# The fifth channel tile of an Infini-attention kernel: summed in one bank per 64-row half instead of in two halves of its columns, with a rewritten order

## The chip, the cores and the metric

The kernel runs on one core of a Trainium2 chip, as one launch. The metric is the device time of one execution in microseconds (us); before the change the median of three runs is 519.08 us (518.57 to 522.13).

## What is computed

A token gate mixes two branches of the same input x (2048 tokens of 640 channels). Branch a is Infini-attention with 32 heads of 20 channels over 4 segments of 512 tokens: within a segment softmax attention with a mask, plus a read of a memory that the earlier segments left. Branch b sends one token through a gated feed-forward network and adds the result to it.

```
q, k, v = (x @ wq, x @ wk, x @ wv), each cut into 32 heads of 20 channels
for s in range(4):                                   # segments of 512 tokens
    p = softmax(qs @ ks.T * scale + mask);  a_dot = p @ vs
    a_mem = (phi(qs) @ M) / (phi(qs) @ z + 1e-6)
    o = g * a_mem + (1 - g) * a_dot
    M += phi(ks).T @ vs;  z += phi(ks).sum()
a = o @ wo;   b = x + (one token through the network)
out = gate * a + (1 - gate) * b
```

## The kernel before, in words

The heads are taken in two halves of 16, and each half runs over the four segments, so the work falls into 8 units, u = 0 to 7. A unit projects x on its queries and keys (channels on the partitions, 512 tokens on the columns), on its values (tokens on the partitions), and runs four groups of four heads through the attention. All projections and the products of queries and keys work with numbers split into a high and a low part: hi*hi, lo*hi and hi*lo are summed, so each product is three matmuls.

TensorE is used as two halves of 64 rows (r = 0 and 1) that run at the same time, with two matmuls that start together (a pair, below). Both may not write one PSUM bank at the same time. PSUM is four pairs of banks (`banks`, 128 x 2 x 512 float32 each); an accumulation takes a whole pair or one bank of it.

The queries and keys of a unit are 640 channels, five tiles of 128. `t_job` (L700) sums them over KT = 5 blocks of input channels: tiles 0 and 1 together ("P1"), 2 and 3 together ("P2"), and tile 4 alone ("T4"). `paired` (L646) issues the matmuls, all of them at L665. It goes over the five blocks twice (`by_phase`): in phase 0 half r writes bank r, in phase 1 it writes bank 1 - r, so that after both phases each bank has the sum over all rows. For P1 and P2 bank b holds tile j0 or j1, with 512 columns. For T4 there is one tile only, so its 512 columns are cut, and bank b holds 256 of them:

```
b = r ^ ph
xh, xl = (t.t[:, 256 * b:256 * b + 256] for t in (xh, xl))        # if j0 == j1
```

Between the phases, the two halves change banks, and no half may write into a bank in which the other is still at work. Where the order gives no other proof of that, a poke is planned (L653): VectorE copies two numbers out of the pair into `nil`, after phase 0, and the first matmul of phase 1 waits for it.

`evac_t` (L767) takes a tile out: ScalarE copies it from PSUM to `xs` (L779; for T4 from both banks, 256 columns each, L777), and the pair is free. For P1 of unit 0 alone, which `first_job` (L675) sums into two pairs, VectorE adds the second pair to `xs` (L782). GpSimdE then rounds `xs` to its high part `hi` (L430) and subtracts to get the low part `lo` (L434), and SyncE's queue sends both to DRAM (`stk`), from where `fetch` (L861) brings them back laid out by head. Behind the first segments `phi` is made from `xs` too (L787 to L789).

The attention's matmuls are L903 (products for the row maxima, which VectorE reduces at L909 and L914), L953 (products for the exponentials, which ScalarE takes at L959), L986 (p @ v), L824 and L845 (the memory's read and write). The feed-forward network runs beside them, and 16 output jobs (`o_job`, 320 columns a matmul) close the program.

Nothing of the order is left to a scheduler. Every operation is a task with a number, the string ORDER lists all tasks in the order in which they are issued (L99 to L199), and BANKS gives the bank of each accumulation as it is opened; `Plan.order` (L307) reads both. Each engine runs its tasks in that order.

Of the kernel before, what the change touches and what calls it, by code (L numbers as in the profile page):

```python
# [103 lines left out]
62 7a 5m 5k 61 6d 7x 6m 6e 5y 6f 3g 55 9s 39 75 7b 56 5o 5z 7c 5n 5r 7d 70 76 6h 7e 53 60 6i 5u 5p 7f 5s 6z 7g 8h 6j 6y b 71
7h 3h 8i 6r 7i 5w 77 8v 7j 78 hh 6k 8w ad 6l 9d 72 ae 7m 9v 6x 7k 73 9e 9w 7n 6w 7l 74 9t 9x 9u 7o 65 7y 7p 9y 67 66 6n is 7z
9z c 7q 5v 68 7r 80 a0 7s a1 69 81 6o 6s 5x 7t 6p a2 7u 3d a3 6q a4 3e 3j 8b 82 3b a5 8c 6a 8d 83 54 bv 8f j ce 6t 8e bw 3c c6
3i 9b 84 57 87 3k bx 9a 88 3l 3m 86 cb 3a 89 85 by 58 59 cj h 99 c7 8a bz cc f cf 8x 98 6u 3n be 8y 3o 3p b3 c0 16e 3q g 8o cg
3r c1 90 b5 6v c2 8p c9 c8 bf 91 b6 c3 8r 92 hi 8j 16c 8s c4 8k 8t ck 9f 8l c5 9g 8m e0 9i e1 9h 8n e2 eb k 93 8z e3 94 ej e4
96 95 8q 9j 9m e5 97 a6 9l e6 9n cl b4 e7 9k e8 9p 9o ca e9 a7 ea ch cd fz ci ga 9q a8 g0 a9 9r g1 ec b7 g2 b8 g3 aa as g4 ba
b9 de g5 ab at g6 ed df ac bb g7 av bd af d bc ek g8 dc eg g9 ag el ii aw al ef ax hd ee ah ai e eo i au he bo am aj bp ak bg  # L110
bm bh ay dg az bi bj b1 b0 eh bn bq di bk dh b2 an dj dk ao cu dd ap dm br bl gb ep hq hj dl fp d1 fn cv cm d2 bs fm h2 bu h3
bt d4 d3 en h4 cn em d5 dn h5 d6 cp co h6 do gc cq h7 du cr h8 dq h9 dv dr eq d7 ha d8 dt dx hb da d9 hr ds hc db ij dy hs er
jn jm aq fw j1 dz es r6 ks ge cs fx eu et ar ft fo ik kt ev ct fu fb fv ey ew id fc j4 dp ex ie j5 dw fe fy j6 ic it ez ff iu
ib f4 fg f1 1b7 j2 gf j3 gg gi f5 f2 j7 gj fd f3 j8 3f gl gv fh j9 gm cw fi f6 ja gw fj go fl cx gp ei jb gy gx fk gn gq jc gd
s9 cy gz fq gs f7 gr jd f8 fr gk fs h1 je h0 f0 gt i0 lm ht gu lu ln i1 lo cz i3 d0 il sj hu lb kg im i4 hk lp lc r7 i5 io ld
r8 hl ip le iq lv hn lf 16f lx lw ir ke ho iv lg jf hp lh iw i2 lq in li f9 iy ix jg i6 lj gh ku fa kh iz ji hm lk j0 jh lz ll
i7 m0 i9 jj i8 hf o6 mz ia jl jk o7 mx if hv ly hw ju hx kf lr hy ls n0 ny lt hg nz k3 ig nn k4 no o1 o0 jv np o9 nq k6 nr o2
jo kl ns ss k7 jp nt hz k8 nu nv jr nw km js nx jt po ko pp pz pq jw q0 kp k9 pr ka kr kn ps kc kb jx ih kq l4 jq rf l1 l5 my
jy ki m1 kd l7 l6 m8 l2 pt mv jz kv l8 pu kw l3 q2 la mw pv m9 l9 o3 pw kx pc px ky k5 py o8 pe kz m2 r2 mb l0 ob oa oc k0 m3
# [78 lines left out]
2l2  # L198
"""  # L199
BANKS = ("624062406064202660264610406400264025046272624620466012402460622006246026061246204226016214602405435620462442604407420654"  # L200
         "224027460462461024260762067602406206205402476046034242064270436742603420440622454623404260542406262462040476256240746054"
         "262043042046432603423760204606246704266023642066235604264406470263460302402654224670362024662612406202432074260205064042"
         "6651562044042000642")

# [1123 lines left out]
```

## Time and profile before

| | |
|---|---|
| median of three runs | 519.08 us (518.57 to 522.13) |
| the profiled execution | 519.61 us |
| its span, first to last instruction | 517.9 us |
| granted TensorE clock over the span | 0.998 |
| PE busy | 508.5 us, 98% |
| weight loads (PEld) busy | 409.7 us, 79% |
| VectorE (DVE), ScalarE (ACT), GpSimdE (POOL) busy | 416.6, 407.4, 335.2 us |

Times in the profile count from the span's start. L12 is line 12 of the kernel. "out<-in" are the program's names for what an instruction writes and reads, without buffer numbers. An idle time is followed by what ended it. PE's matmuls are pipelined and their ends modelled, so a busy PE may still have lost time between two starts; the distance from one start to the next is the better measure of its pace. DVE is VectorE, ACT ScalarE, POOL GpSimdE, SP the queue that issues DMAs.

### The profile page before, as it was taken

How to read it: one execution, taken by the hardware profiler on the slowest of the kernel's cores; microseconds unless marked ns; L12 is line 12 of the kernel's file. 1: busy time of each engine (PE TensorE's matmuls, PEld its weight loads, DVE VectorE, ACT ScalarE, POOL GpSimd, SP SyncE). 2: the span in 40 equal slices, each digit the busy share in tenths (PEclk: the TensorE clock that was granted, in tenths of full speed). 3: DMA queues.
4: the chain of work that ended last, by engine and by line, in shares of the span. 5: the costliest groups of instructions: out<-in, count | busy, mean ns of one | idle time of the engine just before them, and what ended most of it. 6: DMA issues, size and time to landing. Idle time of an engine off the chain costs nothing.

```text
span 517.9 us, 17296 instructions
## 1 busy us (share of the span) xinstructions
PE 508.5 (98%) x6916; PEld 409.7 (79%) x6916; DVE 416.6 (80%) x727; ACT 407.4 (79%) x701; POOL 335.2 (65%) x439
## 2 busy tenths in 40 slices
PE   8999999999999999999999999999999999999996
PEld 5998967877777877687778777777778688787896
...
GB/s 253 266 258 212 205 218 223 195 261 212 146 187 255 243 213 244 235 261 242 248 256 230 290 257 216 297 244 235 252 295 213 263 251 251 241 162 183 188 161 130
DMA packets 57712, 119.02 MB, mean 230 GB/s; under 512 B 6240, under 2 KB 13920, under 8 KB 57632
## 3 DMA queue, kind: packets, MB, share of 16 engines
...
## 4 chain that ended last, share of the span: by engine, by line
PE 89%; DVE 3%; DMA 2%; ACT 2%; POOL 1%; issue 1%; SPq 0%; DVEq 0%; ACTq 0%; POOLq 0%
PE bank L665 49%; PE bank L986 13%; PE bank L953 8%; PE bank L903 7%; PE bank L824 4%; PE bank L845 3%; DMA ffn<-in_wg_dram 1%; PE bank L806 1%; ACT pt L959 1%; PE bank L691 1%; DVE mx L914 1%; DMA pt<-in_xT_dram 1%; POOL pt L961 1%; DVE pt L1212 1%; PE bank L926 1%
## 5 line engine op out<-in xcount | busy, mean ns | idle before, releaser
L959 ACT ACTIVATE pt<-bank 128x1024 f32<-128x1024 f32 x160 | 163.1, 1023 | 43.9 <-PE bank L953 39.5
L914 DVE TENSOR_REDUCE mx<-bank 128x2 f32<-128x256 f32 (+2 forms) x192 | 160.8, 859 | 24.1 <-PE bank L903 17.0
L961 POOL TENSOR_SCALAR_AFFINE_SELECT pt<-pt 128x512 f32<-128x512 f32 (+1 forms) x160 | 96.4, 618 | 66.5 <-ACT pt L959 65.1
L665 PE MATMUL bank<-xhi,whi 64*128 64x512 f32 (+1 forms) x460 | 87.8, 364 | 0.0
L665 PE MATMUL bank<-xhi,wlo 64*128 64x512 f32 (+1 forms) x460 | 84.6, 350 | 0.6 <-DVE wlo L434 0.6
L896 ACT CAST bank<-cau 128x512 f32<-128x512 bf16 (+1 forms) x160 | 81.0, 508 | 5.0 <-PE bank L894 1.5
L665 PE MATMUL bank<-xlo,whi 64*128 64x512 f32 (+1 forms) x460 | 84.7, 351 | 0.0
L434 POOL TENSOR_TENSOR xlo<-raw,xhi 128x512 fp32r<-128x512 f32 x53 | 69.5, 1323 | 22.4 <-ACT xhi L428 16.0
L986 PE MATMUL bank<-pt,va 128*32 128x512 f32 (+3 forms) x1024 | 75.5, 435 | 0.6 <-POOL pt L961 0.6
L953 PE MATMUL bank<-qs,ks 62*128 62x256 f32 (+3 forms) x512 | 68.7, 327 | 1.9 <-ACT kk L811 0.8
L903 PE MATMUL bank<-ks,qs 60*128 60x512 f32 (+3 forms) x512 | 69.5, 321 | 0.0
L986 PEld LDWEIGHTS bank<-pt,va 128*32 128x32 f32 x1024 | 30.4, 110 | 43.4 <-issue 34.0
L665 PE MATMUL bank<-vhi,xhi 64*128 64x322 f32 (+1 forms) x320 | 56.6, 323 | 0.1
L953 PEld LDWEIGHTS bank<-qs,ks 62*128 62x128 f32 x512 | 45.6, 185 | 12.9 <-issue 2.6
L665 PE MATMUL bank<-vlo,xhi 64*128 64x322 f32 (+1 forms) x320 | 53.9, 307 | 0.0
L665 PE MATMUL bank<-vhi,xlo 64*128 64x322 f32 (+1 forms) x320 | 53.9, 307 | 0.0
L434 POOL TENSOR_TENSOR lo<-xs,hi 128x512 fp32r<-128x512 f32 x40 | 53.0, 1327 | 1.3
L903 PEld LDWEIGHTS bank<-ks,qs 60*128 60x128 f32 x512 | 47.4, 186 | 6.6 <-ACT bank L896 1.4
L665 PE MATMUL bank<-whi,xhi 64*128 64x320 f32 x320 | 51.0, 312 | 0.0
L665 PEld LDWEIGHTS bank<-xlo,whi 64*128 64x128 f32 x460 | 46.5, 184 | 5.2
L665 PEld LDWEIGHTS bank<-xhi,wlo 64*128 64x128 f32 x460 | 46.8, 186 | 4.5 <-POOL wlo L434 0.8
L665 PE MATMUL bank<-whi,xlo 64*128 64x320 f32 x320 | 50.0, 305 | 0.0
...
## 6 DMA issues: line engine op xcount, KB each, us to landing
stk<-hi SPq DMA_DIRECT2D x40, 512.0 KB
...
```

The source lines that it names most:

```text
L434: plan.add(engine, dur, lambda: e.tensor_tensor(out=lo, in0=src, in1=f32(hi), op=OP.subtract), key, [*reads, hpart], [lpart], lazy=engine ...
L665: nc.tensor.matmul(t[:, b, :n], w[64 * r:64 * r + 64], m[64 * r:64 * r + 64], start=i == 0 and p == 0, stop=ends and p == 2, skip_group_ch ...
L691: nc.tensor.matmul(t[:, b, c], w[k].t[64 * r:64 * r + 64, 128 * b:128 * b + 128], m.t[64 * r:64 * r + 64, c], start=k == 0 and p == 0, sto ...
L824: nc.tensor.matmul(t[32 * j:32 * j + 32, ps.bank, :], mbd.t[:, g, 32 * j:32 * j + 32], e.t, start=True, stop=True)
L845: nc.tensor.matmul(t[32 * m:32 * m + 32, ps.bank, :GW], kk.t[:, g, c, 32 * m:32 * m + 32], v.t[:, c, GW * pos:GW * pos + GW], start=c == 0 ...
L896: act(key, acts(256 * d), lambda: nc.scalar.copy(sub(banks[ps.pair], at_, [[512, 2], [pitch, d], [1, 128]]), sub(cau.t, 0, [[0, 2], [0, d] ...
L903: nc.tensor.matmul(a[:, b, to:to + w], q.t[64 * b:64 * b + ST, p, 128 * i:128 * i + 128], sub(k.t[64 * b:64 * b + ST], L * p + 384, [[-128 ...
L914: dve(key - TOP, 0.15 + 2 * w / 960.0, lambda p=p, i=i, to=to, w=w: nc.vector.tensor_reduce(out=sub(m_.t, 4 * p + i, [[8, 2], [1, 1]]), in ...
L953: nc.tensor.matmul(sub(bt, 512 * b + to, [[pitch, w // 128], [1, 128]]), k.t[64 * b:64 * b + ST + 2, p, 128 * c:128 * c + 128], q.t[64 * b ...
L959: act(key - EXPS, 0.22 + 2 * 512 / 1270.0, lambda: nc.scalar.activation(pt.t, banks[ps.pair], AF.Exp, scale=SCALE), [ps], [pt])
L961: pool(key, 0.42 if len(parts) == 1 else 0.64, lambda: nc.gpsimd.affine_select(out=d, in_=d, pattern=[[0, 2], [0, len(parts)], [1, 128]], ...
L986: nc.tensor.matmul(o[32 * j:32 * j + 32, ps.bank, L - w:], v.t[:, c, VW * h:VW * h + 32], sub(t.t, 512 * (j // 2) + to, [[pitch, 4 - c], [ ...
```

## The change

T4 is no longer cut and no longer goes through `paired`. Half r of the rows writes bank r of the pair all along, with all 512 columns; there is one phase of five steps, and no poke. Each bank then holds the sum over half of the rows, and the two must be added: ScalarE copies bank 0 to `xs`, and VectorE adds bank 1 to it, with the addition that P1 of unit 0 has. What follows (`hi`, `lo`, `stk`, `phi`) is the same. The strings ORDER and BANKS are written anew.

```diff
@@ t_job
         ps = Ps("proj")
+        if j0 == j1:
+            for k in range(KT):
+                def whole(k=k):
+                    xh, xl = (x.t for x in X[u, k])
+                    wh, wl = (w[k].t[:, 128 * j0:128 * j0 + 128] for w in (whi, wlo))
+                    for p, (w, m) in enumerate(((wh, xh), (wl, xh), (wh, xl))):
+                        for r in range(2):
+                            nc.tensor.matmul(banks[ps.pair][:, r, :], w[64 * r:64 * r + 64], m[64 * r:64 * r + 64],
+                                             start=k == 0 and p == 0, stop=k == KT - 1 and p == 2, skip_group_check=True)
+                pe(key + span * k / KT + LATER, 3 * stream(L) + 0.01, whole, [*X[u, k], *((w[k], p) for w in (whi, wlo) for p in sorted(WPARTS[j0]))],
+                   [ps], opens=ps if k == 0 else None)
+            at(key + span + 0.01, lambda: evac_t(u, j0, ps, None, key + span))
+            return
         steps = by_phase()
...
-            if j0 == j1:
-                xh, xl = (t.t[:, 256 * b:256 * b + 256] for t in (xh, xl))
...
@@ evac_t
-        def copy():
-            t = banks[ps.pair]
-            if b is None:
-                nc.scalar.copy(sub(xs.t, 0, [[256, 2], [1, 256]]), sub(t, 0, [[512, 2], [1, 256]]))
-            else:
-                nc.scalar.copy(xs.t, t[:, b, :])
-        act(key - COPY, acts(L), copy, [ps, *more], [xs])
-        for o in more:
-            dve(key - COPY, 0.7, lambda: nc.vector.tensor_tensor(out=xs.t, in0=banks[o.pair][:, b, :], in1=xs.t, op=OP.add), [xs, o], [xs])
+        act(key - COPY, acts(L), lambda: nc.scalar.copy(xs.t, banks[ps.pair][:, b or 0, :]), [ps, *more], [xs])
+        for o, c in [(o, b) for o in more] if b is not None else [(ps, 1)]:
+            dve(key - COPY, 0.7, lambda o=o, c=c: nc.vector.tensor_tensor(out=xs.t, in0=banks[o.pair][:, c, :], in1=xs.t, op=OP.add), [xs, o], [xs])
@@ ORDER, BANKS: every line rewritten, the first of each shown in part
-y l 4 m n o p r 5 q z 0 t 24 s 26 1e 25 1c v 27 18 u 1a 19 3s 7 x 3t
-BANKS = ("624062406064202660264610406400264025046272624620466012402460622006246026061246204226016214602405435620462442604407420654"
+BANKS = ("224062416062402042060407664066240620641021206024622547046204022405426402445740264066234274062464520420622060426265260245"
```

In the changed kernel the lines move a little: L665 is L663, the new matmuls are L711, L691 is L689, L903 is L904, L953 is L954, L986 is L987, L845 is L846, L806 is L807, L914 is L915, and the addition L782 is L783. Over the whole program PE has 240 matmuls of 512 columns for T4 where it had 480 of 256; VectorE has 10 additions where it had 2, and 42 pokes where it had 49; the tasks of ScalarE, GpSimdE and SyncE are as many as before. PE's 32 blocks of L986 stand at nearly the same places in both orders.

PE before, the end of T4 of unit 6 (its pair is bank0, the number behind a name is the buffer's) and what follows it until the pair is opened again:

```order
L665 MATMUL bank0_65<-xlo3_105,whi3_79 128x256 x2
L903 MATMUL bank3_68<-ks2_122,qs2_118 128x384 x2
L903 MATMUL bank3_68<-ks2_122,qs2_118 128x128 x2
L665 MATMUL bank0_65<-xhi4_100,whi4_80 128x256 x2
L665 MATMUL bank0_65<-xhi4_100,wlo4_85 128x256 x2
L665 MATMUL bank0_65<-xlo4_106,whi4_80 128x256 x2
L806 MATMUL bank1_66<-identf_70,phi1_138 128x64 x4
L845 MATMUL bank1_66<-va1_125,kk_126 32x84 x16
L903 MATMUL bank2_67<-ks2_122,qs2_118 128x512 x2
L953 MATMUL bank3_68<-qs1_117,ks1_121 128x384 x2
L953 MATMUL bank3_68<-qs1_117,ks1_121 128x128 x2
L953 MATMUL bank0_65<-qs1_117,ks1_121 128x512 x2
```

PE in the changed kernel, the same place (the pair is bank3):

```order
L711 MATMUL bank3_68<-xlo3_105,whi3_79 128x512 x2
L904 MATMUL bank0_65<-ks2_122,qs2_118 128x384 x2
L904 MATMUL bank0_65<-ks2_122,qs2_118 128x128 x2
L711 MATMUL bank3_68<-xhi4_100,whi4_80 128x512 x2
L711 MATMUL bank3_68<-xhi4_100,wlo4_85 128x512 x2
L711 MATMUL bank3_68<-xlo4_106,whi4_80 128x512 x2
L846 MATMUL bank2_67<-va1_125,kk_126 32x84 x16
L807 MATMUL bank2_67<-identf_70,phi1_138 128x64 x4
L904 MATMUL bank1_66<-ks2_122,qs2_118 128x512 x2
L954 MATMUL bank0_65<-qs1_117,ks1_121 128x384 x2
L954 MATMUL bank0_65<-qs1_117,ks1_121 128x128 x2
L954 MATMUL bank3_68<-qs1_117,ks1_121 128x512 x2
```

The two tasks of L845 and L806 have changed places; otherwise what stands between the tile's last matmul and the next opening of its pair (L953, 512 columns) is the same six rows.

DVE before, from the poke of that T4 (nil) on:

```order
L653 COPY nil_73<-bank0_65 1x2
L1098 SCALAR_TENSOR_TENSOR fgu_69<-ffn0_155,xrow_183,fgu_69 128x448
L914 TENSOR_REDUCE mx0_148<-bank1_66 128x2 x2
L1009 STREAM_TRANSPOSE on0_141<-nt2_144 128x512
L914 TENSOR_REDUCE mx0_148<-bank3_68 128x2 x2
L1033 COPY jp_74<-top1_176 1x128
L854 TENSOR_TENSOR mt_128<-bank1_66,mask4_72 128x84
L789 SCALAR_TENSOR_TENSOR phi2_139<-xs3_132,phi2_139 128x512
L914 TENSOR_REDUCE mx0_148<-bank2_67 128x2
```

DVE in the changed kernel, the same stretch (xs2 of bank3 is the new addition):

```order
L1099 SCALAR_TENSOR_TENSOR fgu_69<-ffn0_155,xrow_183,fgu_69 128x448
L1002 TENSOR_TENSOR zr1_146<-zr1_146,gts_75 128x16
L915 TENSOR_REDUCE mx0_148<-bank2_67 128x2
L1071 TENSOR_SCALAR sg_182<-sg_182 128x1
L915 TENSOR_REDUCE mx0_148<-bank2_67 128x2
L1006 TENSOR_TENSOR nt2_144<-nt2_144,zr1_146 128x16x20
L915 TENSOR_REDUCE mx0_148<-bank0_65 128x2 x2
L783 TENSOR_TENSOR xs2_131<-bank3_68,xs2_131 128x512
L1072 RECIPROCAL sg_182<-sg_182 128x1
L855 TENSOR_TENSOR mt_128<-bank2_67,mask4_72 128x84
L915 TENSOR_REDUCE mx0_148<-bank1_66 128x2
```

The poke is gone, and the addition stands behind the reductions of the row maxima (L915) and ahead of the write of the memory (L855) and the next reduction.

PE before, at the start of the program, T4 of unit 0 (bank0) and P1 (bank1 and bank2) over the second block of channels (xhi1):

```order
L691 MATMUL bank2_67<-xhi1_97,whi1_77 128x512 x2
L691 MATMUL bank2_67<-xhi1_97,wlo1_82 128x512 x2
L691 MATMUL bank2_67<-xlo1_103,whi1_77 128x512 x2
L691 MATMUL bank1_66<-xhi0_96,wlo0_81 128x256 x2
L665 MATMUL bank0_65<-xhi1_97,whi1_77 128x256 x2
L665 MATMUL bank0_65<-xhi1_97,wlo1_82 128x256 x2
L665 MATMUL bank0_65<-xlo1_103,whi1_77 128x256 x2
L665 MATMUL bank3_68<-xhi1_97,whi1_77 128x512 x2
L665 MATMUL bank3_68<-xhi1_97,wlo1_82 128x512 x2
L665 MATMUL bank3_68<-xlo1_103,whi1_77 128x512 x2
L691 MATMUL bank1_66<-xhi1_97,whi1_77 128x512 x2
```

PE in the changed kernel, the same place:

```order
L689 MATMUL bank2_67<-xhi1_97,whi1_77 128x512 x2
L689 MATMUL bank2_67<-xhi1_97,wlo1_82 128x512 x2
L689 MATMUL bank2_67<-xlo1_103,whi1_77 128x512 x2
L689 MATMUL bank1_66<-xhi1_97,whi1_77 128x512 x2
L689 MATMUL bank1_66<-xhi1_97,wlo1_82 128x512 x2
L689 MATMUL bank1_66<-xlo1_103,whi1_77 128x512 x2
L711 MATMUL bank0_65<-xhi1_97,whi1_77 128x512 x2
L711 MATMUL bank0_65<-xhi1_97,wlo1_82 128x512 x2
L711 MATMUL bank0_65<-xlo1_103,whi1_77 128x512 x2
```

The step of T4 over the second block now comes behind P1's six pairs over that block instead of ahead of three of them.

## Rows read from the trace of the kernel before

**Rows 1.** The page, its part 1: busy time of each engine, its share of the span, and how many instructions it ran.

```profile
PE 508.5 (98%) x6916; PEld 409.7 (79%) x6916; DVE 416.6 (80%) x727; ACT 407.4 (79%) x701; POOL 335.2 (65%) x439
```

**Rows 2.** Busy time in three stretches, start:end in us; the columns are the length, the busy time of PE, PEld, DVE, ACT and POOL with their instructions, the granted clock, the DMA share and GB/s.

```profile
0.00:20.00 20.00, 17.88 (x165) 14.55 (x167) 12.53 (x27) 13.41 (x36) 14.30 (x23) 1.00 0.80 250
60.00:450.00 390.00, 386.96 (x5390) 300.71 (x5388) 332.07 (x576) 335.76 (x568) 263.47 (x339) 1.00 0.78 239
500.00:518.00 18.00, 13.71 (x188) 13.44 (x184) 9.62 (x18) 3.02 (x5) 0.00 (x0) 0.95 0.41 148
```

**Rows 3.** The page, its part 4: shares of the chain that ended last, by engine and by line.

```profile
PE 89%; DVE 3%; DMA 2%; ACT 2%; POOL 1%; issue 1%; SPq 0%; DVEq 0%; ACTq 0%; POOLq 0%
PE bank L665 49%; PE bank L986 13%; PE bank L953 8%; PE bank L903 7%; PE bank L824 4%; PE bank L845 3%; DMA ffn<-in_wg_dram 1%; PE bank L806 1%; ACT pt L959 1%; PE bank L691 1%; DVE mx L914 1%; DMA pt<-in_xT_dram 1%; POOL pt L961 1%; DVE pt L1212 1%; PE bank L926 1%
```

**Rows 4.** The end of the chain that ended last, in order of time: start, us, what.

```profile
489.31 20.89 PE bank L665 x282
...
510.23 0.90 DVE pt L1212
...
511.26 0.81 DVE pt L1201
...
512.16 2.48 DVE pt L1212 x3
```

**Rows 5.** PE in order of time, the fifth tile of u = 4 and what follows it: start, us, line, op, out<-in, rows*columns, shape of the moving operand, count.

```profile
221.56 0.28 PE L665 MATMUL bank<-xhi,wlo 64*128 64x256 f32 x2
...
223.09 0.28 PE L665 MATMUL bank<-xlo,whi 64*128 64x256 f32 x2
223.21 0.40 PE L953 MATMUL bank<-qs,ks 62*128 62x512 f32 x2
223.45 0.40 PE L903 MATMUL bank<-ks,qs 60*128 60x256 f32 x4
223.69 0.41 PE L665 MATMUL bank<-vhi,xhi 64*128 64x320 f32 x2
223.94 0.31 PE L665 MATMUL bank<-vlo,xhi 64*128 64x320 f32 x2
224.08 0.31 PE L665 MATMUL bank<-vhi,xlo 64*128 64x320 f32 x2
```

**Rows 6.** PE in order of time, the start of the program.

```profile
9.35 0.33 PE L665 MATMUL bank<-xhi,whi 64*128 64x256 f32 x2
10.32 0.39 PE L665 MATMUL bank<-xhi,wlo 64*128 64x256 f32 x2 [0.64 <-DVE wlo L434]
...
12.01 0.44 PE L691 MATMUL bank<-xhi,whi 64*128 64x512 f32 x2
...
15.91 0.52 PE L691 MATMUL bank<-xlo,whi 64*128 64x512 f32 x2
```

**Rows 7.** Groups by shape of the projections: PE matmuls of 256 columns (all of the fifth tile), and one of the three kinds of weight load; busy us, mean ns.

```profile
L665 PE MATMUL bank<-xhi,whi 64*128 64x256 f32 x160 | 24.0, 285 | 0.0
L665 PE MATMUL bank<-xhi,wlo 64*128 64x256 f32 x160 | 23.4, 277 | 0.6 <-DVE wlo L434 0.6
L665 PE MATMUL bank<-xlo,whi 64*128 64x256 f32 x160 | 23.3, 277 | 0.0
L665 PEld LDWEIGHTS bank<-xhi,whi 64*128 64x128 f32 x460 | 46.6, 185 | 3.8 <-DVE wlo L434 0.8 <-DVE mr L932 0.2
```

**Rows 8.** Groups by shape on ScalarE and VectorE that read PSUM: busy us, mean ns | idle before, and who ended it.

```profile
L777 ACT COPY xs<-bank x8: 579/584/630, 26.6 to 382.0; 128x512 f32<-128x512 f32 x8
L782 DVE TENSOR_TENSOR xs<-bank,xs 128x512 f32<-128x512 f32 x2 | 1.4, 680 | 0.1
L653 DVE COPY nil<-bank x49: 136/147/150, 18.9 to 511.1; 1x2 f32<-1x2 f32 x49
L914 DVE TENSOR_REDUCE mx<-bank 128x2 f32<-128x1024 f32 x64 | 77.9, 1217 | 13.4 <-PE bank L903 9.0 <-ACT xhi L428 1.4 <-ACT pt L959 1.1
```

**Rows 9.** Who waited for whom: us in total, times, longest.

```profile
DVE nil L653 <- PE bank L665: 22.7, 22, 5.0
PEld bank L953 <- DVE mx L914: 1.5, 4, 0.8
POOL hi L430 <- ACT xs L777: 5.5, 2, 4.4
```

**Rows 10.** PE, ScalarE and VectorE in order of time, around the end of the fifth tile of u = 6.

```profile
329.80 0.29 PE L665 MATMUL bank<-xlo,whi 64*128 64x256 f32 x2
329.93 0.40 PE L806 MATMUL bank<-identf,phi 64*128 64x64 f32 x4
330.26 0.79 PE L845 MATMUL bank<-va,kk 128*32 128x84 f32 x32
330.98 0.50 PE L903 MATMUL bank<-ks,qs 60*128 60x512 f32 x2
331.32 0.68 PE L953 MATMUL bank<-qs,ks 62*128 62x384 f32 x6
330.42 0.58 ACT L777 COPY xs<-bank 128x512 f32<-128x512 f32 x1
329.79 1.29 DVE L914 TENSOR_REDUCE mx<-bank 128x2 f32<-128x256 f32 x2
```

More of the change, by code (lines that the diff above doesn't have):

```diff
@@ L104 @@
[L104 to L119, printed above, removed]
@@ L196 @@
[L196 to L203 removed]
+y l 0 4 m n o p r 5 q 26 z 24 v 27 s 1c 1e 1 t 1d 18 u 1f 19 3s 3t 15u 1a x 25 3v 1i w 3u 1b 3w 3y 3x 1k 3z 1j 40 42 1g 10 5a
@@ new lines @@
+1ci 1c9 16n 1ds 1aa 174 13w 1d1 17s 1dt 16r 13x 17t 1a7 175 1e2 1d2 1fa 1at 1e3 176 1nn 16s 1go 177 1ch 179 17f 1au 16t 172
+17v 178 1ck 1gp 195 1eq 17a 1b8 1es 16u 17g 196 1or 1er 17w 1cj 1ba 189 1et 198 16w 18a 1eu 17x 1cn 199 1bc 1dq 1ev 197 17y
+18c 19a 17u 192 1ew 1a8 1cl 14g 18d 18b 19b 19w 193 1cm 19n 18e 19x 19z 1b9 1cp 13y 19h 19o 1a0 1bb 1ey 19i 1a1 1dp 1ez 19k
+19j 1ab 1co 19l 1ad 1bm 1ac 1f0 19m 1ea 1bn 1do 1f1 194 1bp 1bs 1a2 1f2 1a3 1bt 1a5 1a4 19p 1bq 16v 1h5 1a6 1br 1bv 1h6 1p3
@@ new lines @@
+1hg 1dn 1bw 1cq 16x 1h7 1hh 16y 1bd 1bf 1cr 1hj 1h8 1ho 1bx 1bg 1h9 1by 1bu 1ae 1ec 1bi 1cs 1ha 1be 1hi 1hb 1ag 1eb 1ct 1af
+1dc 1ee 1bj 1dd 1cu 1g0 1hc 1hp 1bk 1hk 1hq 1hd 1df 1bl 1cv 1du 1dg 1bh 1he 1hs 1dh 1cx 16z 1bo 1hf 1dv 1hr 19y 1cy 1ed 17h
+16c 1d3 1k8 1cz 1eh 1dw 1dx 1nz 1kg 1k9 1fz 1hl 1ef 1gw 1d4 1di 1eg 1m1 1dj 1ht 1m2 1dl 19q 1gx 1m3 1d5 1hu 1kh 1ej 1dk 1m4
+1d6 19r 1hm 1kb 19s 1m5 1dm 1kd 1e4 1dy 1m6 1ei 1de 1cb 1e5 1m7 1e0 1g3 1m8 1hn 1cc 1ki 1g2 1e7 1m9 1ke 1dz 1f3 1e8 1kj 1f4
@@ new lines @@
+1ma 1e9 1mb 1cw 1kk 1k3 1e6 1f6 1g1 1f5 1kf 1ni 1k4 1d8 1ek 1f7 16d 19t 1fo 1no 1fh 1el 1fp 1f8 1f9 1fr 1np 1g5 19u 1em 1fb
+1fi 1g4 1fs 1ka 1k5 1fc 1ft 1g7 1k6 1pf 19v 1fe 1k7 1fj 1kl 1kc 1en 1eo 1d7 1gh 1j2 1fk 1ff 1mc 1d9 1n7 1gi 1md 1j0 1n8 1n9
+1fg 1me 1ig 1gk 1fq 1ih 1fu 1na 1fl 1fv 1g8 1gq 1fx 1fw 1g6 1nb 1gr 1fy 1gl 1gy 1nc 1g9 1nd 1gn 1ga 1da 1gt 1ne 1gz 1nf 1gm
+1db 1gu 1gs 1o0 1gc 1ng 1fd 1gv 1j3 1h1 1ls 1gj 1nh 1lu 1h2 1h0 1lt 1j1 1q2 1ia 1h3 1ip 1lr 1ib 1ii 1hv 1lp 1iq 1h4 1ic 1gb
@@ L709, in operands @@
             j = (j0, j1)[b]
-            xh, xl = X[u, k]
+            xh, xl = (x.t for x in X[u, k])
             wh, wl = (w[k].t[:, 128 * j:128 * j + 128] for w in (whi, wlo))
-            if j0 == j1:
-                xh, xl = (t.t[:, 256 * b:256 * b + 256] for t in (xh, xl))
-            else:
-                xh, xl = xh.t, xl.t
             return (wh, xh), (wl, xh), (wh, xl)
@@ L720, in reads_of @@
             return [*X[u, k], *((w[k], p) for w in (whi, wlo) for p in sorted(parts))]
-        paired(ps, steps, operands, L if j0 != j1 else 256, lambda i: key + span * i / len(steps), reads_of, "T")
-        for i, j in enumerate((j0, j1) if j0 != j1 else (j0,)):
-            at(key + span + 0.01, lambda i=i, j=j: evac_t(u, j, ps, None if j0 == j1 else i, key + span))
+        paired(ps, steps, operands, L, lambda i: key + span * i / len(steps), reads_of, "T")
+        for i, j in enumerate((j0, j1)):
+            at(key + span + 0.01, lambda i=i, j=j: evac_t(u, j, ps, i, key + span))
     def v_job(u, c, key, span):
```

170 lines of the change are left out of this document (87 added, 83 removed).

## The prediction

> **What bounds the kernel now.** I read the busy shares first, then the stretches, then the chain that ended last, then PE in order of time at three places, and last the groups and waits of the engines that empty PSUM. PE is busy 98% of the span, VectorE 80%, ScalarE 79% [rows 1]. The stretches say where PE is not busy: it is 386.96 of 390 us from 60 to 450, so 3.04 us are open there; 2.12 us are open in the first 20 us and 4.29 in the last 18 [rows 2]. The chain is 89% PE, 49% of it the projections of L665, with no other engine above 3% [rows 3]. The granted clock is 1.00 in the first two of these stretches [rows 2], so that is the upper of the two levels, 2.4 GHz, and no gain from the clock is to be had there. The end is PE up to about 510, then VectorE's last combinations, which end at 512.16 + 2.48 = 514.64 [rows 4]. So the time is a stream of PE's starts plus a few waits, and the change is priced by how long that stream becomes and which waits come or go.
>
> **The change part by part.**
>
> PE's stream. T4 of one unit is 30 pairs of 256 columns before and 15 pairs of 512 after; there are 8 units, so 240 pairs become 120 (the groups show 3 x 160 matmuls, that is 240 pairs [rows 7]). The mean durations of these rows (277 to 285 ns) overlap and are no pace; the pace is the distance of starts. In T4 of u = 4 the pair that starts at 221.56 and the one at 223.09 are 13 pairs apart: 1.53 / 13 = 0.118 us a pair [rows 5]. For 512 columns, the pairs of L691 from 12.01 to 15.91 are 18, or 17 steps: 3.90 / 17 = 0.229 us [rows 6]. So 240 x 0.1177 = 28.2 us become 120 x 0.2294 = 27.5: **-0.7 us**. The number of columns is the same, and half as many instructions save almost nothing, because the pace of 256 columns is already 0.51 of that of 512.
>
> Here a rule speaks for a larger gain. The rows show a weight load of 185 ns in each group [rows 7], and pairs at 0.118 us, so the loads lie beside the matmuls. The Trainium skill, "TensorE: Matmul & The Clock Gate", Part 3 (Packing small matmuls), says that a weight load overlaps a running matmul only where the row group differs; its Part 2 gives a load of 128 columns as about 107 ns. If every pair paid that in the open, 240 pairs would cost 25.7 us of loads and 120 half of it, an estimate of -12.8 us from that page. The trace disagrees, since 0.118 us a pair leaves no room for 0.107 in the open.
>
> The start. T4's second step waits 0.64 us at 10.32 for the low part of the weights [rows 6]. In the rewritten order that step comes behind all six pairs of P1 over the second block instead of ahead of three of them. Three more pairs of 0.229 us, 0.69, come ahead of it, just more than the wait. Bounds: 0, if the weights come as late as PE is early, and -0.64; I take **-0.6**.
>
> The pair of banks. Before, ScalarE's copy frees both banks: 584 ns [rows 8]. After, the pair is free when VectorE's addition has ended, 680 ns of its own by the two additions that exist [rows 8], and it can't begin before the copy's end. At u = 6 the last matmul of T4 ends at 329.80 + 0.29 = 330.09, the copy runs from 330.42 to 331.00, and the pair is opened again by the last two of the six matmuls that begin at 331.32, thus about 331.6 [rows 10]. An addition straight behind the copy ends near 331.00 + 0.68 + 0.1 = 331.8, and PE would wait 0.2 us. By the order the work between tile and reopening is the same before and after at u = 6, and elsewhere of similar length. Bounds: 0, where PE comes back later; 8 x 0.68 = 5.4 where every addition stands bare in PE's way, and more where VectorE has a reduction in hand at that time (below, as a rival). At six to eight places some pay 0.2 and most nothing: I take **+0.4**.
>
> VectorE's load. Eight additions more are 8 x 0.68 = +5.4 us, seven pokes less are 7 x 0.147 = -1.0 [rows 8] and, since a poke waits for PE (22.7 us over all 49 [rows 9]), 7 x 0.46 = -3.2 us of waiting. The cover is VectorE's idle time, 20% of the span [rows 1]; with 80% + 0.9% it doesn't become the bound. If the cover were gone, the net +1.2 us would be the price. I take 0. Behind the addition in VectorE's queue at u = 6 stand the memory's write (L855) and the next reduction; the engine that waits for these is PE at L954, which before waited 1.5 us in 4 times for reductions [rows 9]. The reduction of 1024 columns is 1217 ns [rows 8].
>
> The poke's other side. A poke keeps PE from starting phase 1 too early; seven of them go, but PE's idle time holds no wait for them that I could find in the middle stretch, so nothing is won.
>
> Latency of the tile. `hi` waits for `xs`, which is finished 0.7 us later or, with the queue of VectorE, some 2 us later. GpSimdE waited only 5.5 us in 2 times for T4's copy [rows 9], has 35% of its time free [rows 1], and the tile's data go through DRAM and back before anything reads them. The cover is that distance of many microseconds; I take 0, with +0.5 as the bound.
>
> The rewritten order. Blocks of different kinds of matmul follow each other as before: the runs of instructions from one line grow from 647 to 657. The first pair of a new run can take longer: at 223.69 to 223.94 it is 0.25 us against 0.14 of the next [rows 5]. Ten more of 0.10 are at most +1.0; I take **+0.3**. The waits in the middle stretch are 3.04 us in all. The places where PE can wait (the blocks of L986 for their exponentials) stand at nearly the same spots, so I carry these 3.04 us over. Bounds: -3.0, if all went, and about +4, if the new order left as many again.
>
> The sum: -0.7 - 0.6 + 0.4 + 0.3 = **-0.6 us**. The profiled execution took 519.61, so its counterpart would be 519.0. That execution is 0.53 above the median of 519.08, so the forecast is **518.5**. One per cent, 5.2 us, is about what a measurement of this kernel can tell from no change; the forecast is no change.
>
> **The rivals.**
>
> (a) Faster through the order. All 3.04 us of the middle stretch's waits and the start's 0.64 go, the stream gives its 0.7, and nothing is paid: 519.08 - 4.4 = 514.7 us; with as much from the pace behind line changes (now shorter runs elsewhere) it passes 513.9. For it: the order was rewritten throughout, not only at T4. Against it: the waits that are left are few and small, and stand where the data's latency sets them.
>
> (b) Slower through the held pair. The copy and then the addition hold the pair, and VectorE takes its work in order. If the addition comes up while a reduction of 1.22 us [rows 8] is in hand, or stands in the queue ahead of one and waits for ScalarE, the pair comes free 1.2 us later than in my sum, or the reduction frees its own bank late. With seven units (in u = 0 PE has other work): 7 x 1.2 = 8.4 in place of 0.4, so 518.5 + 8.0 = 526.5. It decides from the point where the addition ends later than about 1.5 us behind the tile's last matmul, which is the distance at u = 6 (330.09 to 331.6 [rows 10]). For it: at that very place VectorE ran two reductions from 329.79 to 331.08 [rows 10], so its queue is not empty. Against it: the order puts the addition behind the reductions that are due first, and PE in front of a closed bank is something that an order can move away from. The Trainium skill, "TensorEngine Tiling (Array Packing)", Gotcha 1 (PSUM Pressure), warns in this direction: row tiling takes more banks, as different row tiles may not write the same bank at once. No run so far shows what it costs here.
>
> (c) Loads in the open. If the weight loads of T4 do cost time that the pace of one stretch hides, the gain is that of 120 loads; at the row's 185 ns [rows 7], 22 us at most, at half of it 11, so some 508. For it: 120 loads fewer. Against it: the pace of 0.118 us. The page that would have it so is named above.
>
> (d) The change doesn't do what it says: T4 runs at 512 columns, but the two halves no longer run beside each other, because both read the same tile. Then a pair would cost 0.46 us and T4 27 us more, 546. Against it: P1 of unit 0 has just that form (two halves, two banks, 512 columns), and runs at 0.229 us a pair [rows 6].
>
> **How the numbers follow.** The forecast's case, within some 3 us of 518.5, gets 0.62. (a) gets 0.17, of which about 0.11 is past 1%. (b) gets 0.18, of which 0.15 is past 1%; (c) 0.02; (d) 0.01. Faster by over 1% is (c) and the far part of (a): 0.13; slower by over 1% is (b)'s and (d)'s: 0.16, and a little from unknown waits, 0.18; within 1% 0.69. The range reaches down to (a) with all waits gone and 2.7 us of pace besides, 512.0, and up into (b), to nearly all of its places paid, 526.0; some 2 in 10 lie outside, half of it on each side. The likeliest case alone is 516 to 521.
>
> **What would show it.** In the changed kernel's profile: T4's pairs of L711 start every 0.229 us, and L711's matmuls are 240 (stream). At the start, the wait for the low part at T4's second step is gone. Around each T4, in order of time, copy and addition follow each other, and the matmul that reopens the pair starts within 0.3 us of when PE could; waits of PE for VectorE's addition sum to under 1 us. VectorE's busy time is 4.4 us higher, and PE's open time from 60 to 450 is 2 to 4 us. The prediction is wrong if that open time is above 7 us with L783 or L915 as what ended the waits (b), below 1 us (a), or if T4's pairs have another pace than 0.229 us (c, d).

## The result, and the profile after

The changed kernel takes 523.3 us (median of 14 runs, 521.73 to 528.97) where the kernel before takes 520.0 (median of 14, 518.57 to 522.62; the forecast's 519.08 is the median of the first three of them). The ratio is 1.0065, 95% interval 1.0038 to 1.0091: slower by 3.3 us, where 0.6 us less was forecast. In a second series it was 523.5 beside 520.3, ratio 1.0052 (1.0032 to 1.0073).

The profiled execution took 521.74 us with a span of 519.8, so it is one of the fastest of its kernel and shows 2.1 of the 3.3 us. Its busy times, and then its three stretches (length, busy time of PE, PEld, DVE, ACT, POOL with their instructions, granted clock, DMA share, GB/s), beside [rows 1, 2]:

```profile
PE 509.0 (98%) x6676; PEld 401.7 (77%) x6676; DVE 425.8 (82%) x728; ACT 407.4 (78%) x701; POOL 336.6 (65%) x439
```

```profile
0.00:20.00 20.00, 18.66 (x152) 12.86 (x154) 12.85 (x24) 13.83 (x35) 15.85 (x26) 1.00 0.75 237
60.00:450.00 390.00, 384.74 (x5182) 294.78 (x5180) 338.71 (x576) 334.81 (x568) 267.31 (x343) 1.00 0.78 238
500.00:520.00 20.00, 15.71 (x216) 15.45 (x212) 9.73 (x18) 3.43 (x5) 0.00 (x0) 0.95 0.40 142
```

PE's open time from 60 to 450 us grew from 3.04 to 5.26 us, above the 2 to 4 that were expected, while it shrank from 2.12 to 1.34 at the start and is the same 4.29 at the end. The granted clock is that of before in each stretch. VectorE has 9.2 us more, twice the 4.4 that the working gave. PE's waits show who ends them; the columns are the sum, how often, the longest, in us:

```profile
PE bank L954 <- DVE mr L933: 1.4, 1, 1.4
PE bank L954 <- DVE nt L991: 0.9, 1, 0.9
PE bank L987 <- DVE mx L915: 0.9, 1, 0.9
PE bank L954 <- DVE mx L910: 0.7, 1, 0.7
PE bank L711 <- DVE mx L915: 0.4, 1, 0.4
PE bank L954 <- DMA qs<-mr: 0.4, 1, 0.4
PE bank L904 <- ACT bank L897: 0.2, 1, 0.2
```

Five of these seven waits are put down to VectorE, 4.3 us of 4.9 (both kernels have another of 1.3 us at the very start, left out here). In the kernel before, PE's waits for VectorE behind the first 20 us are two:

```profile
PE bank L926 <- DVE mt L854: 0.3, 1, 0.3
...
PE bank L953 <- DVE nt L990: 0.2, 1, 0.2
```

One of the five is a DMA's, the 0.9 us for L991. The matmul that waits starts at 113.78 us, and it needs the DMA `qs<-mr` besides, which landed at 113.65. In the second profile of the changed kernel (below) the same matmul waits 1.45 us, by the view for L828. But there the DMA landed at 114.37, and the weight load started 0.11 us later, before L828 ended at 114.50:

```profile
114.48 0.33 PEld L954 LDWEIGHTS bank<-qs,ks 62*128 62x128 f32 x4 [1.62 <-DVE nt L991]
```

```profile
113.83 0.67 DVE L828 STREAM_TRANSPOSE nt<-bank 128x512 f32<-128x512 f32 x1
```

In four of the experiments the view names the DMA at this matmul, with 0.56 to 1.19 us. So 3.4 us of the 4.9 are VectorE's. None is for the addition (L783). What answers to [rows 5] is T4 of u = 4, PE in order of time:

```profile
222.82 0.40 PE L711 MATMUL bank<-xhi,whi 64*128 64x512 f32 x2
...
223.98 0.40 PE L711 MATMUL bank<-xlo,whi 64*128 64x512 f32 x2
```

Five steps in 1.16 us, 0.232 us a pair, where 0.229 was reckoned. To [rows 8, 9] answers the addition, with its count and durations (min, median, max in ns); one weight load waited 0.2 us for it:

```profile
L783 DVE TENSOR_TENSOR xs<-bank,xs x10: 674/688/692, 17.2 to 379.4; 128x512 f32<-128x512 f32 x10
```

And to [rows 10] the end of T4 of u = 6, PE, then ScalarE, then VectorE:

```profile
332.43 1.09 PE L954 MATMUL bank<-qs,ks 62*128 62x384 f32 x6
```

```profile
331.44 0.59 ACT L781 COPY xs<-bank 128x512 f32<-128x512 f32 x1
```

```profile
331.09 1.28 DVE L915 TENSOR_REDUCE mx<-bank 128x2 f32<-128x256 f32 x2
332.29 0.68 DVE L783 TENSOR_TENSOR xs<-bank,xs 128x512 f32<-128x512 f32 x1
```

The copy ends at 332.03, the addition comes up 0.26 us later behind the reductions, and ends at 332.97. PE's two matmuls that reopen the pair are the last of the six from 332.43, a row that takes 1.09 us where 0.68 stood in [rows 10]. So 0.4 us are lost at this place, where 0.2 were reckoned.

### The profile page after: what moved, and what is told of

It reads as the page before. It is cut to its first block, busy times and chain, and to the rows that moved or that the text cites. A ratio compares the mean times of both kernels' runs of the same rounds, so it can differ in the third digit from the quotient of the medians.

```text
span 519.8 us, 16822 instructions
## 1 busy us (share of the span) xinstructions
PE 509.0 (98%) x6676; PEld 401.7 (77%) x6676; DVE 425.8 (82%) x728; ACT 407.4 (78%) x701; POOL 336.6 (65%) x439
## 4 chain that ended last, share of the span: by engine, by line
PE 89%; DVE 6%; DMA 2%; issue 2%; ACT 1%; DVEq 0%; ACTq 0%
PE bank L663 43%; PE bank L987 13%; PE bank L954 8%; PE bank L904 7%; PE bank L711 5%; PE bank L825 4%; PE bank L846 3%; DVE mx L915 2%; PE bank L807 1%; PE bank L689 1%; PE bank L553 1%; DMA ffn<-in_wu_dram 1%; DMA qs<-mr 1%; DVE mx L910 1%; PE bank L927 1%
## 5 line engine op out<-in xcount | busy, mean ns | idle before, releaser
L915 DVE TENSOR_REDUCE mx<-bank 128x2 f32<-128x768 f32 (+2 forms) x192 | 160.6, 859 | 19.9 <-PE bank L904 16.3
L962 POOL TENSOR_SCALAR_AFFINE_SELECT pt<-pt 128x512 f32<-128x512 f32 (+1 forms) x160 | 93.1, 598 | 66.6 <-ACT pt L960 58.9
L432 POOL TENSOR_TENSOR xlo<-raw,xhi 128x512 fp32r<-128x512 f32 x53 | 71.5, 1359 | 13.0 <-ACT xhi L426 10.4
L987 PE MATMUL bank<-pt,va 128*32 128x512 f32 (+3 forms) x1024 | 75.4, 435 | 1.0 <-DVE mx L915 0.9
L954 PE MATMUL bank<-qs,ks 62*128 62x256 f32 (+3 forms) x512 | 69.5, 325 | 3.5 <-DVE mr L933 1.4
L904 PE MATMUL bank<-ks,qs 60*128 60x384 f32 (+3 forms) x512 | 69.5, 322 | 0.2 <-ACT bank L897 0.2
L987 PEld LDWEIGHTS bank<-pt,va 128*32 128x32 f32 x1024 | 31.4, 109 | 42.8 <-issue 34.0
L663 PE MATMUL bank<-xhi,whi 64*128 64x512 f32 x300 | 63.4, 409 | 0.0
L663 PE MATMUL bank<-xlo,whi 64*128 64x512 f32 x300 | 60.6, 390 | 0.0
L663 PE MATMUL bank<-xhi,wlo 64*128 64x512 f32 x300 | 60.4, 389 | 0.0
L954 PEld LDWEIGHTS bank<-qs,ks 62*128 62x128 f32 x512 | 45.8, 185 | 15.1 <-DVE mr L933 2.5
L663 PE MATMUL bank<-vhi,xhi 64*128 64x322 f32 (+1 forms) x320 | 56.2, 323 | 0.0
L904 PEld LDWEIGHTS bank<-ks,qs 60*128 60x128 f32 x512 | 46.5, 186 | 10.0 <-ACT bank L897 3.9
L663 PE MATMUL bank<-vhi,xlo 64*128 64x322 f32 (+1 forms) x320 | 53.6, 307 | 0.0
L663 PE MATMUL bank<-vlo,xhi 64*128 64x322 f32 (+1 forms) x320 | 53.5, 307 | 0.0
L663 PE MATMUL bank<-whi,xhi 64*128 64x320 f32 x320 | 51.8, 312 | 0.0
L663 PE MATMUL bank<-wlo,xhi 64*128 64x320 f32 x320 | 50.7, 305 | 0.0
L663 PE MATMUL bank<-whi,xlo 64*128 64x320 f32 x320 | 50.7, 305 | 0.0
L910 DVE TENSOR_REDUCE mx<-bank 128x4 f32<-128x1024 f32 x32 | 38.8, 1211 | 5.4 <-PE bank L904 5.2
## 6 DMA issues: line engine op xcount, KB each, us to landing
stk<-hi SPq DMA_DIRECT2D x40, 512.0 KB
```

The costliest lines, as they stand in the source:

```text
L432: plan.add(engine, dur, lambda: e.tensor_tensor(out=lo, in0=src, in1=f32(hi), op=OP.subtract), key, [*reads, hpart], [lpart], lazy=engine ...
L663: nc.tensor.matmul(t[:, b, :n], w[64 * r:64 * r + 64], m[64 * r:64 * r + 64], start=i == 0 and p == 0, stop=ends and p == 2, skip_group_ch ...
L904: nc.tensor.matmul(a[:, b, to:to + w], q.t[64 * b:64 * b + ST, p, 128 * i:128 * i + 128], sub(k.t[64 * b:64 * b + ST], L * p + 384, [[-128 ...
L910: dve(key - TOP, 0.15 + 2 * 512 / 960.0, lambda: nc.vector.tensor_reduce(out=sub(m_.t, 1, [[4, 4], [1, 1]]), in_=sub(banks[ps.pair], 0, [[ ...
L915: dve(key - TOP, 0.15 + 2 * w / 960.0, lambda p=p, i=i, to=to, w=w: nc.vector.tensor_reduce(out=sub(m_.t, 4 * p + i, [[8, 2], [1, 1]]), in ...
L954: nc.tensor.matmul(sub(bt, 512 * b + to, [[pitch, w // 128], [1, 128]]), k.t[64 * b:64 * b + ST + 2, p, 128 * c:128 * c + 128], q.t[64 * b ...
```

## What the three waits on VectorE have ahead of them

Three of the waits for VectorE come back in all four profiles of the new order in which VectorE's order and GpSimdE's work are unchanged (the changed kernel twice, and two of the experiments below). Ahead of each stands an operation of VectorE that takes far longer than the same operation elsewhere. The kernel before has such operations too (the counterpart of L1006 takes up to 1.49 us there), but the two waits of 0.3 and 0.2 us are all that PE has for VectorE behind its first 20 us. Near 227 us (VectorE, then GpSimdE, then PE; the bracket is the wait):

```profile
224.62 1.63 DVE L790 SCALAR_TENSOR_TENSOR phi<-xs,phi 128x512 f32<-128x512 f32 x1
226.17 1.21 DVE L910 TENSOR_REDUCE mx<-bank 128x4 f32<-128x1024 f32 x1
```

```profile
224.41 1.29 POOL L432 TENSOR_TENSOR lo<-xs,hi 128x512 fp32r<-128x512 f32 x1
```

```profile
227.44 0.50 PE L954 MATMUL bank<-qs,ks 62*128 62x256 f32 x4 [0.65 <-DVE mx L910]
```

`phi` of L790 takes 1.63 us; its shortest in this profile is 0.63. GpSimdE's subtraction lo = xs - hi began 0.21 us before it and ended at 225.70, and `phi` ended 0.55 us after that. The reduction L910 stands behind it in VectorE's queue, and PE waits 0.65 us for L910. Near 409 us it is the gate's L1067, 1.54 us for 16 columns (0.633 in the profile before), beside GpSimdE's L1103:

```profile
406.73 1.54 DVE L1067 TENSOR_SCALAR gb<-gx 128x16 f32<-128x16 f32 x1
...
408.35 0.27 DVE L933 SCALAR_TENSOR_TENSOR mr<-bank,mr 16x128 fp32r<-16x128 f32 x1
```

```profile
406.18 2.07 POOL L1103 TENSOR_TENSOR fgu<-ffn,fgu 128x640 f32<-128x640 f32 x1 [1.11 <-ACT ffn L1102]
```

```profile
408.67 0.50 PE L954 MATMUL bank<-qs,ks 62*128 62x384 f32 x4 [1.37 <-DVE mr L933]
```

Near 213 us it is two, L1002 (1.11 us, its shortest 0.16) beside GpSimdE's subtraction and L1006 (1.07 us, its shortest 0.42) beside L1008. They stand ahead of the reduction L915, for which L987 waits 0.90 us:

```profile
210.52 1.07 DVE L1006 TENSOR_TENSOR nt<-nt,zr 128x320 f32<-128x320 f32 x1
211.51 1.21 DVE L915 TENSOR_REDUCE mx<-bank 128x2 f32<-128x1024 f32 x1
```

```profile
210.48 0.76 POOL L1008 TENSOR_TENSOR nt<-nt,zr 128x320 f32<-128x320 f32 x1
```

```profile
212.87 1.39 PE L987 MATMUL bank<-pt,va 128*32 128x512 f32 x12 [0.90 <-DVE mx L915]
```

The Trainium skill, "SBUF — State Buffer", Who interferes with whom, says that a VectorE instruction with two inputs in SBUF contends with a GpSimdE instruction that reads SBUF, that one in a two-port mode, which a copy and a tensor_scalar can enter, contends with GpSimdE as well, and that whichever issues first has the shared pair of ports for its whole length. The traces agree, though they don't show in which mode an instruction ran, and a copy of one row of 128 numbers (L1034) shows it best. In the first profile of the changed kernel it began 0.11 us ahead of GpSimdE's subtraction, in the second 0.03 us behind it:

```profile
190.01 0.22 DVE L1034 COPY jp<-top 1x128 f32<-1x128 f32 x1
```

```profile
190.12 1.30 POOL L432 TENSOR_TENSOR xlo<-raw,xhi 128x512 fp32r<-128x512 f32 x1
```

```profile
191.10 1.35 DVE L1034 COPY jp<-top 1x128 f32<-1x128 f32 x1
```

```profile
191.07 1.30 POOL L432 TENSOR_TENSOR xlo<-raw,xhi 128x512 fp32r<-128x512 f32 x1
```

It took 0.22 us in the one and 1.35 in the other, and in the second PE waited 0.84 us at 193.13 for the transpose L828 behind it. So at this place 0.84 us of an execution hang on which of two engines comes first, by a tenth of a microsecond or less.

## The experiments

All ratios are to the kernel before, run on the same chip in the same series; the last two moves below (the gate alone, a fourth) ran on another chip than the other experiments. Edits of the order are given in outline, with the tasks' numbers. Where ORDER has another number of lines than in the changed kernel, the lines of the code move by 4 to 6 (L954 is L949 or L947, L783 is L778).

**The changed kernel again** (no edit).

> The changed kernel once more, for a second profile and on one chip with the next three. Ratio to before 1.004 to 1.009, some 523.4 us beside 520.0. Theory O (the rewritten order): of the waits of PE between 60 and 450 us, those for VectorE's reductions and maxima come again at the same places (PE starts that waited near 213, 227, 278 and 409 us in the first profile of the changed kernel), whatever else differs. Theory T (the uncut tile): the waits stand where a pair of T4 is opened again.

523.5 us, 1.0052 (1.0032 to 1.0073). Its profile is of an execution of 524.62 us. PE's open time from 60 to 450 us is 7.78 us there, above the 7 that the prediction named as a sign of being wrong, though only in part for the waits named with it:

```profile
60.00:450.00 390.00, 382.22 (x5148) 294.59 (x5148) 335.50 (x572) 333.24 (x565) 265.33 (x340) 1.00 0.79 238
```

Three waits came again, with the same sizes (0.89 at 214.90, 0.65 at 229.46, 1.34 at 411.25):

```profile
PE bank L954 <- DVE nt L828: 2.3, 2, 1.5
PE bank L954 <- DVE mr L933: 1.3, 1, 1.3
...
PE bank L987 <- DVE mx L915: 0.9, 1, 0.9
...
PE bank L954 <- DVE mx L910: 0.7, 1, 0.7
```

Of the 2.3 us put down to L828, 1.45 are the DMA's at 114 us (above) and 0.84 those behind the copy. The one near 278 did not, so of the four that were named it is three that hold. None stands where a pair of T4 is reopened.

**Old order, T4 uncut.** T4's place in the order of a unit, and VectorE's:

```diff
 ORDER and BANKS of before, the tasks under the changed kernel's numbers
-T4   k0 k1 k2 k3 k4 (phase 0)  poke  k0 k1 k2 k3 k4 (phase 1)    3 pairs of 256 each
+T4   -  k0 -  k1 -             -     k2 -  k3 -  k4              3 pairs of 512 each
 ACT  copy of T4
+DVE  xs + second bank
```

> The order and the banks of before, with T4 uncut: its five steps stand where the second, fourth, ... tenth of its ten steps stood, its pokes are left out, and VectorE's addition stands where VectorE came free after the copy in the profile of before (or just ahead of the reopening of its pair). Theory O: the uncut tile itself costs nothing, T4's stream gives 0.5 us back and some additions cost some tenths: 519 to 521 us, ratio 0.998 to 1.002. Theory T: what is slow is the uncut tile with its addition, so ratio 1.004 to 1.009 with the old order too, 522 to 524.5 us.

526.24 us, 1.0117 (1.0089 to 1.0145). It lies above both theories' ranges, 2.7 us slower than the changed kernel. So in this order the uncut tile does cost time, as theory T said, and more. What it waits for is what the second rival of the prediction named:

```profile
  PE bank L949: 1.7, 2
  PE bank L982: 1.5, 1
...
  PE bank L841: 0.4, 1
```

That is 3.6 us in four places; weight loads wait besides. At 231.46 the addition stands behind an operation of the network (L1094, 1.70 us where its median is 0.87), and L987's counterpart waits 1.46 us for the pair. L1094 began 0.28 us behind a subtraction of GpSimdE (1.29 us from 228.74), so this longest wait is a stretch too:

```profile
229.02 1.70 DVE L1094 SCALAR_TENSOR_TENSOR fgu<-ffn,xrow,fgu 128x640 f32<-128x640 f32 x1
230.64 0.68 DVE L778 TENSOR_TENSOR xs<-bank,xs 128x512 f32<-128x512 f32 x1
```

```profile
231.46 1.92 PE L982 MATMUL bank<-pt,va 128*32 128x512 f32 x18 [1.46 <-DVE xs L778]
```

The places of the additions were chosen for the experiment; other places in the old order were not tried.

**New order, T4 cut.**

```diff
 ORDER and BANKS of the changed kernel, code of before
-T4   k0       k1       k2    k3          k4                      3 pairs of 512 each
+T4   k0 k1    k2 k3    k4    k0 k1       k2 k3 k4                3 pairs of 256, phase 1 from the second k0
+DVE  poke, halfway between k4 and the second k0
-DVE  xs + second bank
```

> The order and the banks of the changed kernel, with T4 cut as before: its ten steps of 256 columns stand at the five places of the new steps (2, 2, 1, 2 and 3 at a place, in u = 0 1, 1, 1, 2 and 5), its eight pokes halfway between fifth and sixth step, no additions. Theory O: still slower than before, ratio 1.004 to 1.009, some 522 to 525 us (a poke or two may cost PE some tenths more). Theory T: as fast as before, 0.998 to 1.002.

525.8 us, 1.0104 (1.0079 to 1.0130). The three waits are there with no addition in the program (0.89 at 215.04, 0.53 at 229.62, 1.31 at 412.73), so they are the order's and not the tile's. New beside them are 1.5 us for pokes (L647), which have no place of their own in this order:

```profile
PE bank L659 <- DVE nil L647: 1.5, 3, 1.1
...
PE bank L947 <- DVE mr L926: 1.3, 1, 1.3
...
PE bank L980 <- DVE mx L908: 0.9, 1, 0.9
PE bank L947 <- DVE mx L903: 0.5, 1, 0.5
```

So each order fits its own form of the tile best: old with old is 1 and with the new form 1.0117, new with new is 1.0065 or 1.0052 and with the old form 1.0104, of which the pokes' 1.5 us are 0.003. The new order is slower than the kernel before with either form.

**A small addition.**

```diff
-nc.vector.tensor_tensor(out=xs.t, in0=banks[o.pair][:, c, :], in1=xs.t, op=OP.add)
+nc.vector.tensor_tensor(out=xs.t[:, :8], in0=banks[o.pair][:, c, :8], in1=xs.t[:, :8], op=OP.add)    # T4 alone
```

> The changed kernel with T4's addition over 8 columns of 512 in place of all (the rest of T4's second bank is left out of the sum): 8 x 0.6 = 4.6 us less for VectorE, and the pair of banks free 0.6 us sooner. Theory O: the additions are not what is slow by themselves, but a shorter queue of VectorE takes some off each wait: ratio to before 1.002 to 1.006, 521 to 523 us. Theory T: 0.997 to 1.001, 519 to 520.5 us.

522.68 us, 1.0043 (1.0022 to 1.0064): 0.8 us less than the changed kernel in its series, as theory O had it. That is what the additions cost in the new order, with VectorE's time and the held pair taken together; the intervals overlap, so the 0.8 is rough. The three waits stayed (0.93, 0.66 and 1.33 us).

**Three tasks of VectorE moved.** VectorE's tasks alone, by the line of the changed kernel:

```diff
 near 210 us
-xt   L1006  nt times zr
 10z  L915   reduction
+xt   L1006
 near 224 us
+15j  L790   phi
 12w  L915   reduction
-15j  L790
 144  L910   reduction
 near 407 us
-16f  L1067  gate
 22u  L855
 23d  L933   mr
 22x  L991   transpose
+16f  L1067
```

> The changed kernel with three tasks of VectorE moved in its order and nothing else: the multiplication of nt (L1006) that starts at 210.5 us behind the reduction after it, the phi of L790 that starts at 224.6 ahead of the reduction of 223.5, and the gate's L1067 that starts at 406.7 behind the transpose of 408.6. Theory O2: the waits of PE near 213, 227 and 409 us (0.9, 0.65 and 1.35 us, in all four profiles of the new order) are these three tasks' doing and lie on the path: PE doesn't wait there any more, and the time falls by 1.5 to 3 us, to 520.5 to 522, ratio 1.000 to 1.004. Rival: the same data are late next for another reason, the waits come back within some us, and the ratio stays at 1.004 to 1.008.

520.25 us, 0.9993 (0.9974 to 1.0011): all of it came back, a little more than was expected. The profile caught the slowest of its 13 executions, 524.33 us, and there the waits for VectorE are nearly gone, and most of what is left is DMAs, the longest the one at 114 us:

```profile
PE bank L949 <- DMA qs<-mr: 3.5, 6, 1.2
...
PE bank L949 <- DMA raw<-in_wc_dram: 0.8, 1, 0.8
...
PE bank L658 <- DVE mx L910: 0.5, 1, 0.5
```

**The gate alone moved.**

```diff
-16f  L1067  gate
 22u  L855
 23d  L933   mr
 22x  L991   transpose
+16f  L1067
```

> The changed kernel with one task moved, the gate's L1067 near 407 us, behind the transpose of 408.6. Theory O2: of the 3.3 us this gives back its own wait alone, 1.35 us: ratio 1.002 to 1.005, 521.3 to 522.8 us, the waits near 213 and 227 us as before. Rival: one of the three moves does it all (0.998 to 1.001), or none of the wait is on the path (1.005 to 1.008).

522.34 us, 1.0020 (0.9994 to 1.0046). The wait near 409 went and the other two stayed, 0.90 and 0.65 us; between 1.0052 or 1.0065 and this lie 1.7 to 2.3 us, which agrees with its own 1.35 within the intervals.

**A fourth move.**

```diff
-     L1034  copy of 1 x 128
 ...  L828   transpose
+     L1034
```

> As three_moved, and the first of the two copies of L1034 (1 row of 128 numbers, 0.22 us in the first profile of the changed kernel and 1.35 us in the second) behind the transpose L828 that follows it. Theory O2 with P: the wait of PE near 193 us (0 in the first profile, 0.84 in the second) goes, and with it some of the scatter: median 519.3 to 520.3, ratio to before 0.997 to 1.000. Rival: nothing more, 0.999 to 1.002.

520.45 us, 1.0004 (0.9984 to 1.0024), with the three moves before it: nothing beyond the third. It doesn't beat the kernel before. No wait stands near 193 in its profile, but none stood in the first profile of the changed kernel either, so whether the move took scatter away is not shown. The gate's operation behind the transpose takes 0.55 us, in place of 1.54:

```profile
408.70 0.55 DVE L1062 TENSOR_SCALAR gb<-gx 128x16 f32<-128x16 f32 x1
```

**Old order, pair not held.**

```diff
-in0=banks[o.pair][:, c, :]    reads [xs, o]
+in0=xs.t                      reads [xs]       # T4 alone
```

> The old order with T4 uncut, as above, but the eight additions read xs twice in place of the pair's second bank (the second half of the rows is left out of the sum), so that ScalarE's copy alone frees the pair; VectorE does as much. Theory H (the pair held by the addition): PE's waits for L778 (3.6 us in 4 places) go, and 526.2 falls to 521.5 to 523, ratio 1.002 to 1.006. Rival (VectorE's added time is what counts, not the pair): 525 to 527, ratio 1.009 to 1.013.

522.07 us, 1.0038 (1.0017 to 1.0059). VectorE does its eight additions still (5.5 us), and 4.2 us are gone: in the old order it is the held pair that costs most. The 1.0038 that is left, some 2 us, is not the held pair's; that VectorE's added time costs it is not shown.

**The subtraction replaced by a fill.**

```diff
-POOL  lo = xs - hi        (reads two tiles of SBUF)
+POOL  memset(lo, 0.0)     (reads none)
```

> The changed kernel with GpSimdE's subtraction lo = xs - hi of the 40 tiles replaced by a fill of lo with zeros, which reads no SBUF (the low part of queries and keys is left out). Theory P: VectorE's operations with two operands in SBUF are stretched where GpSimdE reads SBUF beside them: phi of L790, 782 ns in the mean and up to 1.6 us, falls to some 670 ns in the mean, the waits of PE near 213 and 227 us get shorter by 0.5 us or more, the one near 409 (beside GpSimdE's L1103) stays; 520.5 to 522.5 us. Rival: the stretch has nothing to do with GpSimdE's subtraction, L790 stays above 740 ns, and the time at 522.5 to 524.

521.36 us, 1.0020 (0.9997 to 1.0043). The waits near 213 and 227 went, the one near 409 stayed at 1.12 us. Two others, of 0.76 and 0.83 us, stand at 191 and 387 us; ahead of the first is the copy of L1034 again, which began 0.10 us behind another subtraction and took 1.27 us. The mean of `phi`, in the changed kernel and here:

```profile
L790 DVE SCALAR_TENSOR_TENSOR phi<-xs,phi 128x512 f32<-128x512 f32 x38 | 29.5, 782 | 1.5 <-ACT phi L789 1.5
```

```profile
L791 DVE SCALAR_TENSOR_TENSOR phi<-xs,phi 128x512 f32<-128x512 f32 x38 | 27.5, 730 | 1.9 <-ACT phi L790 1.9
```

782 ns fell to 730, not to 670. Nine of the 38 still took over 0.75 us, the longest 1.11 in place of 1.63, and all nine began while another operation of GpSimdE that reads SBUF was running. The gate's operation stands beside L1103, which was not changed, and stayed at 1545 ns. GpSimdE had 36 us less to do in this kernel, so its time is no clean price of the lock; the durations are what tells.

## Why the prediction was wrong

The steps, in their order:

- **PE's stream, -0.7: right in kind.** The pace came out at 0.232 us a pair. From the start of each T4 pair to the next start on PE, waits left out, the sum is 29.4 us before and 28.9 after (28.5 in the second profile), so -0.5 to -0.9. A gain of 11 to 22 us from fewer weight loads, the third rival, did not come.
- **The start, -0.6: the wait went, the gain did not last.** The open time of the first 20 us fell by 0.78 us, but PE's first block of L986 begins at 64.43 before and its counterpart at 64.44 after. In the second profile a wait of 0.22 us stands at 14.29.
- **The pair of banks, +0.4: of the right size.** It is some 0.8 us together with VectorE's time (the small addition, a rough figure); at u = 6 0.4 us were lost where 0.2 were reckoned. The bound of 5.4 was no exaggeration: with the old order, and the additions where the experiment put them, the held pair cost 4.2 us. So the second rival's mechanism was real, and in the new order hardly any of it is left.
- **VectorE's load, 0: this is where the wrong step begins.** "The cover is VectorE's idle time, 20% of the span." From 150 to 420 us VectorE was busy 237 of 270 us before and is 239 after, 88 and 89%, so the cover there was 12%, little more than half of that, and its operations aren't of fixed length. 9.2 us were added where 4.4 were reckoned: eight additions 5.4, seven pokes -1.1, and the rest is operations that got longer (38 `phi` 716 to 782 ns, 2.5 us; the four of L614 333 to 736 ns, 1.6 us; the gate 0.9 us; others both ways).
- **The rewritten order, +0.3: the step that failed.** "The places where PE can wait ... stand at nearly the same spots, so I carry these 3.04 us over." I compared where PE's blocks stand. The open time of that stretch came to 5.26 and 7.78 us in the two profiles. What sets the longest waits for VectorE is what stands ahead of the awaited reduction or maximum in its queue, and there the new order had put operations that GpSimdE's reading stretches, at three places. They cost 0.9 + 0.65 + 1.35 = 2.9 us, nearly the same in the first four profiles of the new order, and moving one operation at each place took the ratio from 1.0065 or 1.0052 to 0.9993, 3.1 to 3.7 us, which agrees with 2.9 within the intervals. The bound of +4 held this; the value taken did not.

Without these three waits the kernel stands at 0.9993 of before, and the forecast was 518.5 / 519.08 = 0.9989. The other terms thus come out right in their sum, within the interval, and the 3.3 us are the order's. One by one they do not: the start's gain is not kept, and the moved order has another wait, at 114 us, that the kernel before lacks. That the sum agrees so closely is in part luck. The range (512.0 to 526.0) held the result, the direction did not. Of the rivals, the slower one named the right engine and the wrong wait: not for the pair, but for reductions behind VectorE's stretched operations.

What is open: waits for DMAs (`qs`, `ks`) differ from one execution to the next (`qs` 1.3 us in the first profile of the changed kernel with the one at 114 us, 3.5 in that with three tasks moved); what sets them was not tried. Nor was it tried whether such moves would also make the order of before faster.
